# Chunk-selected attention with a gated convolution: the channel order moved into the weights, and seven masks transposed by DMA

## The chip, the cores and the metric

The kernel runs on one core of a Trainium2 chip. The metric is the device time of one launch in microseconds. Engines are called TensorE (PE in the profile, PEld for its weight loads), VectorE (DVE), ScalarE (ACT), GpSimd (POOL) and SyncE (SP), which only issues DMAs here.

## What is computed

Two stages in one launch. The first is causal attention over 4 batches, 8 heads, 768 positions and 64 channels, in which each query may look only at six chunks of 32 keys. The chunks are chosen by an upper bound of the score, made from the smallest and largest key of each chunk. The second stage is a gated linear unit over the 512 channels of all heads: a causal convolution of five taps along the sequence gives a gate for each channel, a matrix product gives a value, and their product goes through an output matrix.

```python
k_min = np.min(k_chunks, axis=3); k_max = np.max(k_chunks, axis=3)
ub = np.sum(np.maximum(q[:, :, :, None, :] * k_min[:, :, None], q[:, :, :, None, :] * k_max[:, :, None]), axis=-1)
ub = np.where(causal, ub, -1e9)
top_chunks = np.argsort(ub, axis=-1)[..., -6:]
scores = scale * np.matmul(q, k.transpose(0, 1, 3, 2))
mask = sel & (pos[:, None] >= pos[None, :])          # sel: the key's chunk is one of the six
scores = np.where(mask, scores, -1e9)
attn = softmax(scores);  attn_out = np.matmul(attn, v)
# ... x = attn_out with the heads side by side: (4, 768, 512)
for k in range(5):
    gate_pre += conv_w[k][None, None, :] * xp[:, k:k + S, :]
gate = 1.0 / (1.0 + np.exp(-gate_pre))
val = x @ w_val
out = (gate * val) @ w_out
```

## The kernel before

The 32 heads are worked on as 16 pairs of heads, p = 0 to 15; four pairs make a batch. All operations are listed with a priority (a stage's offset, plus the pair's number times a period, plus a small correction for each pair), and when the kernel is built a scheduler with a table of costs lays them out into one fixed order for each engine. On the chip each engine runs its list in that order and waits for semaphores where it must. The offsets, the period and the corrections are the numbers PERIOD, OFF and DELTA.

The path of one pair: k and q are loaded and transposed by TensorE (L465), copied out by ScalarE (L471, L507), reduced to chunk bounds by VectorE (L477); GpSimd makes small operands of the bounds (L497 to L502); TensorE makes the upper bounds (L583, or L598 for the first four pairs); VectorE finds the top values and compares (L637, L646), which gives NS, 1 where a chunk is **not** selected. NS must be transposed before it can be used as a penalty:

```python
def selT(p=p):                                             # L656
    b = h16(("sel", p))
    for i in range(NIT):                                   # 5 blocks of 128 x 128
        t.nc.tensor.transpose(out=b[:, i * 128:(i + 1) * 128], in_=vv("NS", p)[:, i, :], identity=t.identh)
def mcopy(p=p):                                            # L662, L664
    if p in EARLY:                                         # pairs 0, 1, 2
        t.nc.scalar.copy(out=vv("MT", p), in_=h16(("sel", p))[:, 0:NIT * 128])
    else:
        t.nc.vector.tensor_copy(out=vv("MT", p), in_=h16(("sel", p))[:, 0:NIT * 128])
```

The scores are two matmuls into the same bank, keys by queries (L678) and then the penalty by MT (L683). ScalarE takes the exponential (L692), GpSimd clears the triangle above the diagonal (L700), TensorE multiplies by v with a column of ones beside it (L721), and VectorE divides by that column. The result is written with channel `32*g + c` at place `4*c + g`, so neighbouring results lie four elements apart:

```python
t.nc.vector.reciprocal(out=rc, in_=b[:, :, D])             # L729
t.nc.vector.tensor_tensor(                                 # L731
    out=vv("on", p).rearrange("q t (c g) -> q t g c", g=4)[:, :, 2 * hh:2 * hh + 2, :],
    in0=b[:, :, 0:D].rearrange("p t (g c) -> p t g c", g=2),
    in1=rc.unsqueeze(2).unsqueeze(3).to_broadcast([128, NT, 2, CH]), op=ALU.mult)
```

`on` is transposed into xT, by TensorE and a VectorE copy (L749, L751) for most pairs, by a DMA transpose for pairs 8 to 14:

```python
t.nc.sync.dma_start_transpose(                             # L754
    out=t.xT[:, p % 8, XL:XL + S].rearrange("c (t q) -> c t q", t=NT),
    in_=vv("on", p).rearrange("q t c -> q (t c)"))
```

For the convolution xT goes through a scratch buffer in DRAM, from which XS takes four channels side by side into one partition (L767, L771); with the order above these are four channels 32 apart. TensorE does the convolution by small diagonal matrices WD (L782), built once from the filter. ScalarE takes a tanh (L788); the value matmuls (L805), gating on VectorE (L813) and output matmuls (L829) follow for each batch.

The weights are loaded to suit that order: w_val by its rows in four strided DMAs, w_out plainly.

```python
def w_val():
    for g in range(4):                                     # L404
        t.nc.gpsimd.dma_start(out=t.wval[g::4], in_=t.w_val.rearrange("(ct g c) e -> g c ct e", g=4, c=32)[g])
def w_out():
    t.nc.gpsimd.dma_start(out=t.wout, in_=t.w_out.rearrange("(et e) o -> e et o", e=128))
```

Of the kernel before, what the change touches and what calls it, by code (L numbers as in the profile page):

```python
# [24 lines left out]
KSZ = 5  # L25
NPAIR = B * H // 2
HB = S // 2
NIT = NT - 1
# [8 lines left out]
SELD = ()  # L37
# [17 lines left out]
for _bi, _segs in enumerate(BANKS):  # L55
    for _col, _jt, _q0, _n in _segs:
        for _i in range(_n // 128):
# [5 lines left out]
PERIOD = 13.9888  # L63
OFF = dict(wdg=365.812, wbig=-412.404, cw=-171.479, load=99.454, ktr=-299.337, qtr=-55.458, kev=-11.458,
           qev=-326.891, ksm=126.528, spl=72.03, vc=306.241, ub=-14.489, top=-212.204, selT=13.558, sc=-46.908,
           ex=-168.011, av=44.528, nrm=91.783, tox=64.078, xs=-89.593, conv=-219.578, tanh=-421.807,
           val=121.402, gv=501.114, out=129.892, ev=145.261)
# [4 lines left out]
EARLY = (0, 1, 2)  # L72
# [6 lines left out]
    wdg=(-4.475, 0, -10.764, -1.987, 2.033, 0, -4.785, -2.614, 0.592, 10.315, -0.932, -0.596, 2.165, -5.612,  # L79
        -6.115, 0),  # L80
    wbig=(0.338, 2.284, 2.312, 3.955, 2.284, 0, 2.359, -3.178, 2.348, 0, 0.237, -0.833, 10.937, 1.375, -0.068,
        0.898),
    cw=(0.01, -4.344, 0, 1.42, 0, 7.277, 3.709, 0, -3.806, 2.37, 9.017, 11.085, 2.915, 1.748, 0, -1.313),
    load=(22.853, 10.481, -1.366, 7.693, -4.489, -0.064, -6.203, 1.08, 14.064, 0.698, -6.083, 0, 0.554, 24.497,
        5.961, 1.331),
    ktr=(-6.278, 1.671, -4.686, 0, -13.252, 0.547, -19.631, 0.094, -1.619, 2.825, 0, 13.211, 0.231, -13.505,
        0.169, 0.169),
    qtr=(0, -2.999, -0.198, -1.684, -0.225, -0.932, -0.697, 5.791, -4.056, 7.187, 0, -6.023, -27.874, 5.254,
        -6.599, 0.947),
    kev=(-2.318, 4.593, -0.511, 7.169, 11.289, -10.745, -0.809, -0.098, 3.8, 1.515, -5.151, 0.867, -0.008,  # L90
        15.747, -2.723, -5.794),
    qev=(-9.704, -0.026, 0.872, -1.066, 0.877, 5.395, 2.396, -2.656, 0, -4.807, -7.099, -6.698, -4.553, 0,
        -8.573, -6.812),
    ksm=(2.968, -0.779, 2.961, -10.575, 5.156, -3.959, -6.512, 0, -2.495, 3.887, -3.949, -0.242, 5.945, 0,
        4.26, 3.885),
    spl=(-3.644, -3.121, 5.651, -5.265, -3.696, 0.587, 0, 0.351, 0.614, 0, -7.431, 2.067, 0.052, 0.506, 0.455,
        0.658),
    vc=(3.53, 0.618, 4.312, -7.064, -1.271, -0.473, 0, 0.387, -2.851, -2.778, -2.789, 0, -3.089, 3.743, -5.236,
        -8.41),
    ub=(-34.616, 8.674, -0.111, 8.208, 11.674, 0.278, 0.154, 1.028, 2.508, 0.474, -2.28, 12.479, 5.429, 11.155,  # L100
        0, -14.798),
    top=(4.06, -2.218, -0.108, -2.736, 3.372, -9.606, -2.777, 0.999, 1.18, 0, 0, 0, 0, -2.663, 0.65, -0.836),
    selT=(-1.343, 0.073, -2.18, -4.611, -19.139, -2.18, -2.256, 6.421, 2.399, 0.067, 0.259, 1.354, -1.984,
        -8.687, 6.579, 0),
    sc=(-1.177, -0.248, 7.153, 1.706, 0, 4.855, 99.574, 2.889, 1.671, 36.583, -4.195, -0.864, 2.658, 7.772,
        8.06, 7.651),
    ex=(4.438, 0, -1.857, 5.99, 7.672, 0, 1.657, -13.074, 22.973, 0, 11.497, 6.699, 9.294, 4.96, 1.319, -6.381),
    av=(-4.883, 0, 16.638, 0.808, 0, 3.656, 0, 2.286, 1.2, -10.459, 0.118, 0.868, 25.013, -20.286, -0.281, 0),
    nrm=(-2.191, -0.406, 2.748, -2.782, 8.522, -3.008, -13.003, -5.319, 7.787, -0.467, -7.559, -3.216, -5.567,
        -6.38, 0, 7.101),  # L110
    tox=(-0.01, 0.016, -25.129, -2.88, -33.605, 0, 5.697, 0.185, 0.682, -3.655, 1.506, 1.493, -4.126, -12.409,
        -17.824, -6.189),
    xs=(2.426, 0, 3.278, 5.577, 4.261, 1.209, 2.648, -15.1, 43.407, -10.841, -2.102, 14.6, -8.246, 1.796,
        -6.886, 1.643),
    conv=(0.165, -7.068, 0, -5.659, -9.164, 0, -1.464, 0, -1.805, 0, 5.265, -1.392, -14.961, 2.661, 0.416,
        -0.681),
    tanh=(6.057, -2.286, -6.723, 0.384, -1.984, 5.971, 1.224, -3.37, 5.788, 4.808, 1.33, 5.008, -1.141, -4.153,
        2.266, -4.981),
    val=(0.564, 5.773, 2.94, 5.419, 10.168, -0.349, 6.821, -105.021, -0.454, 0.57, -23.129, -4.226, -7.487,
        -2.814, 0.39, -1.263),  # L120
    gv=(1.881, 0, -6.009, 2.41, -1.491, -5.581, 4.866, 9.739, 6.248, -1.994, -1.479, 3.901, 0.968, 9.442, 0,
        7.848),
    out=(3.397, -6.947, 0, -12.683, 0, -4.985, -1.525, 0.663, -0.041, 1.671, 2.077, -5.383, -1.07, 0.376,
        -4.172, 0.989),
    ev=(-0.48, 0.806, 3.367, -0.002, 3.796, 5.42, -1.238, 7.536, -3.185, 0, 0, -5.746, 4.018, 0.58, 0.732,
        -9.011),
# [186 lines left out]
def graph(off, period, nbuf):  # L313
# [82 lines left out]
    def w_cw():  # L396
        t.nc.sync.dma_start(out=t.cw, in_=t.conv_w.rearrange("k (c d) -> (k c) d", d=32))
    cwl = G.op("cw", "SP", 0.5, key("cw", 0), w_cw, w=[("cw",)], dma=0.1)

    later, last = [], []  # L400
    def w_val():

        for g in range(4):
            t.nc.gpsimd.dma_start(out=t.wval[g::4], in_=t.w_val.rearrange("(ct g c) e -> g c ct e", g=4, c=32)[g])  # L404
    last.append(G.op("wval", "POOL", 2.0, key("wbig", 2), w_val, w=[("wval",)], dma=3.2))

    def w_out():
        t.nc.gpsimd.dma_start(out=t.wout, in_=t.w_out.rearrange("(et e) o -> e et o", e=128))
    last.append(G.op("wout", "POOL", 1.0, key("wbig", 4), w_out, w=[("wout",)], dma=3.2))

    def w_rep():
        for r in range(2):
            t.nc.vector.tensor_copy(out=t.cw4[:, r], in_=t.cw.unsqueeze(2).to_broadcast([80, 32, 2]))
    cwr = G.op("cwrep", "DVE", 0.3, key("cw", 0), w_rep, r=[("cw",)], w=[("cw4",)])

    def w_tr():
        t.nc.tensor.transpose(out=bank("cwT")[:, 0:80], in_=t.cw4.rearrange("p r d b -> p (r d b)"),
                              identity=t.ident[0:80, 0:80])
    G.op("cwT", "PE", 0.15, key("cw", 2), w_tr, r=[("cw4",), ("ident",)], w=[("cwT",)], ps=["cwT"])
# [21 lines left out]
    for p in range(NPAIR):  # L441
# [211 lines left out]
        def selT(p=p):  # L653
            b = h16(("sel", p))
            for i in range(NIT):
                t.nc.tensor.transpose(out=b[:, i * 128:(i + 1) * 128], in_=vv("NS", p)[:, i, :], identity=t.identh)  # L656
        G.op(f"selT{p}", "PE", 0.28, key("selT", p), selT, r=[("NS", p), ("identh",)], w=[("selT", p)],
             war=[("MT", p)], ps=[("sel", p)])
# [6 lines left out]
        G.op(f"mc{p}", *(("ACT", act(640)) if p in EARLY else ("DVE", dve(640, 2))), key("selT", p), mcopy, r=[("selT", p)], w=[("MT", p)], ps=[("sel", p)])  # L665
# [59 lines left out]
        def norm(hh, p=p):  # L725
            def emit():
                b = bank(("av", p, hh))[:, 0:NT * (D + 1)].rearrange("p (t d) -> p t d", t=NT)
                rc = t.rcp[(p * 2 + hh) % 4]
                t.nc.vector.reciprocal(out=rc, in_=b[:, :, D])  # L729

                t.nc.vector.tensor_tensor(  # L731
                    out=vv("on", p).rearrange("q t (c g) -> q t g c", g=4)[:, :, 2 * hh:2 * hh + 2, :],
                    in0=b[:, :, 0:D].rearrange("p t (g c) -> p t g c", g=2),
                    in1=rc.unsqueeze(2).unsqueeze(3).to_broadcast([128, NT, 2, CH]), op=ALU.mult)
            return emit
# [193 lines left out]
def kernel(  # L929
# [18 lines left out]
    def tl(name, shape, dt=FP):  # L948
        return cp.tile(shape, dt, tag=name, name=name)
# [12 lines left out]
    t.cw = tl("cw", [80, 32])  # L962
    t.cw4 = tl("cw4", [80, 2, 32, 2])
# [6 lines left out]
    t.scr = [dr.tile([2, 128, XH], F16, tag=f"scr{i}", name=f"scr{i}") for i in range(4)]  # L970
    t.wval = tl("wval", [128, NCT, DM], F16)
# [47 lines left out]
```

## Time and profile before

| | |
|---|---|
| Time, median of 3 runs | 196.15 us (196.0 to 198.43) |
| Span of the profiled execution | 194.4 us, 7664 instructions |
| Granted TensorE clock | full speed throughout |
| DMA | 37.64 MB, mean 194 GB/s; 82,192 of 92,468 packets under 512 bytes |
| SyncE's DMA queue | 81.9% of the time of 16 DMA engines |

How to read it: a row of the groups gives line, engine, operation, output and inputs with their shapes, the count, then busy time and mean ns of one instruction, then the idle time of the engine just before it and what ended that. Rows of neighbouring instructions of one engine overlap in time (the next one starts while the last is still finishing), so a row's mean is longer than what the engine gives to it; the step from one start to the next is the better measure. The chain is followed back from the last instruction, at each step to whatever released it. A "landing" of a DMA is the time from its issue to the arrival of its data.

### The profile page before, as it was taken

What the parts mean: (1) busy time and instruction counts of PE and PEld (TensorE: products, weight loads), DVE (VectorE), ACT (ScalarE), POOL (GpSimd) and SP (SyncE); (2) the same over time, 40 slices, a digit from 0 to 9 for tenths busy, and PEclk for the clock granted to TensorE, in tenths of its full rate; (3) what the DMA queues carried; (4) which work ended last, traced back from release to release, by engine and by line L of the source; (5) the groups of instructions that cost most, each with busy time, mean ns of one, the idle gap of its engine ahead of it and who ended that gap; (6) DMA issues with size and microseconds to landing.
All of it is one profiled execution on the core that took longest, in us unless ns stands there. A gap on an engine that the chain in (4) does not pass through costs nothing.

```text
span 194.4 us, 7664 instructions
## 1 busy us (share of the span) xinstructions
PE 182.0 (94%) x3026; PEld 121.5 (63%) x3026; DVE 151.5 (78%) x459; ACT 145.3 (75%) x326; POOL 86.0 (44%) x183
## 2 busy tenths in 40 slices
PE   7979999799999989999999999999899999799992
PEld 2766768577667656566677566677658566444540
DVE  4596998999988989987999899699987742714441
ACT  4659999988789579688989764997889898073421
POOL 5236999977462635454456521526362341000000
PEclk9999999999999999999999999999999999999999
DMA  6999999999399949999898998698971396855425
GB/s 145 218 218 205 222 205 200 216 161 284 81 214 237 237 98 222 254 225 227 174 260 172 135 227 227 162 222 229 140 259 63 57 235 184 259 194 185 165 108 216
DMA packets 92468, 37.64 MB, mean 194 GB/s; under 512 B 82192, under 2 KB 87312, under 8 KB 92432
## 3 DMA queue, kind: packets, MB, share of 16 engines
q1 hardware_dynamic: 91328, 36.10, 81.9%
q0 software_dynamic: 1104, 1.05, 3.9%
q8 instruction: 24, 0.39, 0.9%
q14 instruction: 12, 0.10, 0.2%
HBM read 27.34 MB, written 9.47 MB: 189 GB/s over the span
## 4 chain that ended last, share of the span: by engine, by line
PE 52%; DVE 31%; ACT 7%; DMA 4%; issue 3%; POOL 2%; SPq 0%; ACTq 0%; DVEq 0%; POOLq 0%
PE b L829 11%; PE b L805 8%; DVE on L731 7%; DVE km L477 7%; PE b L782 6%; PE b L678 6%; PE b L721 5%; PE b L465 4%; PE b L683 4%; DVE rl L553 3%; ACT P L692 3%; PE b L583 3%; DVE ql L515 3%; DMA XS<-scr 2%; DVE top L637 2%
## 5 line engine op out<-in xcount | busy, mean ns | idle before, releaser
L692 ACT ACTIVATE P<-b 128x512 f16<-128x512 f32 (+1 forms) x192 | 89.6, 605 | 4.9 <-PE b L683 3.0
L700 POOL TENSOR_SCALAR_AFFINE_SELECT P<-P 128x512 f16<-128x512 f16 (+1 forms) x64 | 35.4, 574 | 44.4 <-ACT P L692 44.4
L678 PE MATMUL b<-Qh,Kh 64*128 64x128 f16 (+3 forms) x384 | 41.7, 259 | 1.4 <-DVE on L731 1.2
L683 PE MATMUL b<-MT,E 64*128 64x128 f16 (+4 forms) x352 | 37.6, 255 | 0.1
L477 DVE TENSOR_REDUCE km<-b 128x12 f32<-128x384 f32 x64 | 32.0, 546 | 5.8 <-PE b L465 5.1
L731 DVE TENSOR_TENSOR on<-b,rcp 128x384 f16<-128x384 f32 x32 | 32.8, 1024 | 1.2
L813 DVE SCALAR_TENSOR_TENSOR gv<-g,b 128x384 f16<-128x384 f32 x32 | 17.0, 551 | 14.9 <-PE b L805 14.3
L721 PE MATMUL b<-VA,P 128*128 128x65 f16 x672 | 27.3, 194 | 0.7 <-DVE on L731 0.7
L721 PEld LDWEIGHTS <-P 128*128 128x128 f16 x672 | 24.3, 98 | 5.2 <-issue 3.7
L788 ACT ACTIVATE g<-b 128x384 f32<-128x384 f32 x32 | 14.1, 501 | 17.7 <-PE b L782 17.7
L678 PEld LDWEIGHTS <-Kh 64*128 64x128 f16 x384 | 18.5, 94 | 13.2 <-issue 9.0
L805 PE MATMUL b<-xT,wval 128*128 128x384 f16 x128 | 24.0, 327 | 0.0
L829 PE MATMUL b<-wout,gv 128*128 128x512 f16 x96 | 23.2, 380 | 0.2 <-DVE on L731 0.2
L839 ACT ACTIVATE osb<-b 128x512 f32<-128x512 f32 x21 | 12.7, 613 | 12.6 <-PE b L829 8.8
L683 PEld LDWEIGHTS <-E 64*128 64x128 f16 x352 | 17.9, 94 | 5.8 <-issue 3.1
L471 ACT ACTIVATE Kh<-b 128x384 f16<-128x384 f32 x32 | 16.4, 532 | 4.7 <-PE b L465 2.8
L507 ACT ACTIVATE Qh<-b 128x384 f16<-128x384 f32 x32 | 14.9, 523 | 3.6 <-PE b L465 3.6
L782 PE MATMUL b<-XS,WD 64*32 64x384 f16 x640 | 16.1, 324 | 1.0 <-DMA XS<-scr 1.0
L553 DVE SCALAR_TENSOR_TENSOR rl<-Qh,ql 128x640 f16<-128x640 f16 x16 | 15.4, 964 | 1.9 <-ACT ql L530 1.8
L805 PEld LDWEIGHTS <-wval 128*128 128x128 f16 x128 | 11.3, 98 | 8.3 <-issue 1.1
L497 POOL TENSOR_TENSOR km<-km 128x24 f32<-128x24 f32 x16 | 5.5, 346 | 23.8 <-DVE km L477 23.8
L570 POOL CAST VA<-vn 128x768 f16<-128x768 f32 x16 | 13.7, 864 | 4.1 <-PE b L721 4.1
(86 smaller groups left out, 302.5 us busy)
## 6 DMA issues: line engine op xcount, KB each, us to landing
XS<-scr SPq DMA_DIRECT2D x32, 194.0 KB, 4.1
kn<-in_k_dram SPq DMA_DIRECT2D x32, 192.0 KB, 4.4
qn<-in_q_dram SPq DMA_DIRECT2D x32, 192.0 KB, 4.5
vn<-in_v_dram SPq DMA_DIRECT2D x16, 384.0 KB, 6.0
out_dram<-osb SPq DMA_DIRECT2D x24, 256.0 KB, 2.2
scr<-xT SPq DMA_DIRECT2D x32, 97.0 KB, 3.7
wval<-in_moe_w_val_dram POOLq DMA_DIRECT2D x4, 128.0 KB, 4.7
wout<-in_moe_w_out_dram POOLq DMA_DIRECT2D x1, 512.0 KB, 7.5
```

The source lines that it names most:

```text
L477: t.nc.vector.tensor_reduce(out=vv("km", p)[:, i, w * 12:(w + 1) * 12], in_=bank(("kn", p, w))[:, 0:HB].rearrange("p (c t) -> p c t", t=CH ...
L553: t.nc.vector.scalar_tensor_tensor(out=vv("rl", p), in0=vv("Qh", p)[:, 128:S], scalar=0.0, in1=vv("ql", p), op0=ALU.is_gt, op1=ALU.mult)
L678: nc.tensor.matmul(out=bb[hh][:, col:col + n], lhsT=kh[HP[hh], jt * 128:(jt + 1) * 128], rhs=qh[HP[hh], q0:q0 + n], start=(si == 0), stop= ...
L683: nc.tensor.matmul(out=bb[hh][:, col + m0 - q0:col + n], lhsT=t.E[HP[hh], jt * 128:(jt + 1) * 128], rhs=mt[HP[hh], m0 - 128:q0 + n - 128], ...
L692: t.nc.scalar.activation(out=t.P[p % 2][hh][bi], in_=bank(("s", p, bi, hh))[:, 0:n], func=AF.Exp, scale=0.125 / QS)
L700: t.nc.gpsimd.affine_select(out=ap, in_=ap, pattern=[[0, n], [1, 128]], compare_op=ALU.is_ge, fill=0.0, base=0, channel_multiplier=-1)
L721: t.nc.tensor.matmul(out=b[:, qt, :], lhsT=t.P[p % 2][hh][bi][:, col:col + 128], rhs=vv("VA", p)[:, hh, jt, :], start=(jt == 0), stop=(jt ...
L731: t.nc.vector.tensor_tensor(out=vv("on", p).rearrange("q t (c g) -> q t g c", g=4)[:, :, 2 * hh:2 * hh + 2, :], in0=b[:, :, 0:D].rearrange ...
L782: t.nc.tensor.matmul(out=bank(("cv", p, r))[32 * g:32 * g + 32, 0:HB], lhsT=t.WD[HP[r], k * 16 + (p % 4) * 4 + g, :], rhs=x[HP[r], g * XH ...
L805: t.nc.tensor.matmul(out=k[:, 0:HB], lhsT=t.wval[:, ct, et * 128:(et + 1) * 128], rhs=t.xT[:, (4 * b_ + ct) % 8, XL + w * HB:XL + (w + 1) ...
L813: t.nc.vector.scalar_tensor_tensor(out=vv("gv", 4 * b_ + et)[:, sl], in0=vv("g", 4 * b_ + et)[:, sl], scalar=1.0, in1=bank(("val", b_, et, ...
L829: t.nc.tensor.matmul(out=k, lhsT=vv("gv", 4 * b_ + et)[:, s * 128:(s + 1) * 128], rhs=t.wout[:, et, :], start=(et == 0), stop=(et == NCT - 1))
```

## The change

Two things are changed, and the order of work was then laid out anew.

First, the norm writes its channels in their own order. The regrouping that the convolution needs is put elsewhere: four neighbouring channels `4*c + g` now lie side by side in a partition of XS, and the convolution gives its result with `g` outermost. So the filter's diagonals are built in another order, the columns of w_val are permuted within each block of 128 by four GpSimd copies, and the rows of w_out are loaded by four strided DMAs.

Second, for pairs 9 to 15 the mask NS is transposed into MT by one DMA transpose on SyncE's queue, and not by five TensorE transposes and a VectorE copy.

```diff
-SELD = ()
+SELD = range(9, NPAIR)
-PERIOD = 13.9888
+PERIOD = 13.2487
 # ... nearly all of OFF and DELTA has new numbers
-        t.nc.sync.dma_start(out=t.cw, in_=t.conv_w.rearrange("k (c d) -> (k c) d", d=32))
+        t.nc.sync.dma_start(out=t.cw, in_=t.conv_w.rearrange("k (e q) -> (k e) q", q=128))
     def w_val():
-        for g in range(4):
-            t.nc.gpsimd.dma_start(out=t.wval[g::4], in_=t.w_val.rearrange("(ct g c) e -> g c ct e", g=4, c=32)[g])
+        t.nc.gpsimd.dma_start(out=t.wvn, in_=t.w_val.rearrange("(ct c) e -> c ct e", c=128))
+    def w_perm(ct):
+        return lambda: t.nc.gpsimd.tensor_copy(out=t.wval[:, ct].rearrange("p (e g c) -> p e g c", e=NCT, g=4),
+                                               in_=t.wvn[:, ct].rearrange("p (e c g) -> p e g c", e=NCT, g=4))
     def w_out():
-        t.nc.gpsimd.dma_start(out=t.wout, in_=t.w_out.rearrange("(et e) o -> e et o", e=128))
+        for g in range(4):
+            t.nc.gpsimd.dma_start(out=t.wout[32 * g:32 * g + 32], in_=t.w_out.rearrange("(et c g) o -> g c et o", g=4, c=32)[g])
     def w_rep():
         for r in range(2):
-            t.nc.vector.tensor_copy(out=t.cw4[:, r], in_=t.cw.unsqueeze(2).to_broadcast([80, 32, 2]))
+            t.nc.vector.tensor_copy(out=t.cw4[:, :, r], in_=t.cw.rearrange("p (c g) -> p g c", g=4).unsqueeze(3).to_broadcast([20, 4, 32, 2]))
     def w_tr():
-        t.nc.tensor.transpose(out=bank("cwT")[:, 0:80], in_=t.cw4.rearrange("p r d b -> p (r d b)"),
-                              identity=t.ident[0:80, 0:80])
+        for g in range(4):
+            t.nc.tensor.transpose(out=bank("cwT")[:, 20 * g:20 * g + 20], in_=t.cw4[:, g].rearrange("p r c b -> p (r c b)"),
+                                  identity=t.ident[0:20, 0:20])
+        def mdma(p=p):
+            t.nc.sync.dma_start_transpose(out=vv("MT", p).rearrange("c (t q) -> c t q", t=NIT),
+                                          in_=vv("NS", p).rearrange("q t c -> q (t c)"))
+        if p in SELD:
+            G.op(f"md{p}", "SP", 1.1, key("selT", p), mdma, r=[("NS", p)], w=[("MT", p)], dma=0.8, tail=1.5)
+        # ... else: transposes and copy as before
-                t.nc.vector.tensor_tensor(
-                    out=vv("on", p).rearrange("q t (c g) -> q t g c", g=4)[:, :, 2 * hh:2 * hh + 2, :],
-                    in0=b[:, :, 0:D].rearrange("p t (g c) -> p t g c", g=2),
-                    in1=rc.unsqueeze(2).unsqueeze(3).to_broadcast([128, NT, 2, CH]), op=ALU.mult)
+                t.nc.vector.tensor_tensor(out=vv("on", p)[:, :, hh * 64:(hh + 1) * 64], in0=b[:, :, 0:D],
+                                          in1=rc.unsqueeze(2).to_broadcast([128, NT, D]), op=ALU.mult)
-                                           lhsT=t.WD[HP[r], k * 16 + (p % 4) * 4 + g, :],
+                                           lhsT=t.WD[HP[r], g * 20 + k * 4 + p % 4, :],
```

More of the change, by code (lines that the diff above doesn't have):

```diff
@@ L61 @@
             MT=2, on=2, xT=8, XS=3, g=8, gv=8, osb=4, scr=4)
-PERIOD = 13.9888
[L64 to L67, printed above, removed]
+PERIOD = 13.2487
+OFF = dict(wdg=689.463, wbig=-821.57, cw=-638.386, load=-26.611, ktr=-313.189, qtr=-239.905, kev=166.913,
+           qev=-383.955, ksm=148.208, spl=244.528, vc=540.922, ub=-278.308, top=-291.823, selT=-172.354,
+           sc=-256.234, ex=-198.66, av=-117.315, nrm=263.685, tox=-134.594, xs=14.333, conv=-269.157,
+           tanh=-393.525, val=323.303, gv=522.471, out=327.173, ev=91.258)
 EARLY = (0, 1, 2)
@@ L78 @@
 DELTA = dict(
[L79 to L124, printed above, removed]
@@ L125 @@
-    ev=(-0.48, 0.806, 3.367, -0.002, 3.796, 5.42, -1.238, 7.536, -3.185, 0, 0, -5.746, 4.018, 0.58, 0.732,
-        -9.011),
+    wdg=(-0.259, 11.176, 5.417, 0.077, -1.668, 4.13, 5.35, 1.029, 15.805, 3.045, -3.731, 0, -3.953, 0, 0, 0),
+    wbig=(4.521, -1.173, -4.251, -0.71, -6.836, -7.879, -1.406, -13.108, -0.554, -12.202, 1.098, -1.574,
+        -2.473, -1.919, 10.286, 15.067),
+    cw=(0, 0, 1.049, 0, -3.776, -0.311, -0.92, -4.993, -0.92, -6.529, -7.915, -11.168, 0.948, 0, -8.06, 3.706),
+    load=(-9.433, -20.842, -32.131, -6.001, -15.044, -1.827, -12.02, 13.514, 5.014, 13.589, 14.754, 5.081,
+        -6.414, 4.609, -2.48, -7.659),
@@ new lines @@
+    ktr=(-2.8, -5.035, -2.262, 2.581, 0.902, 9.564, 0, 0, 10.923, 1.13, -0.491, -0.903, 0, 13.091, 0, -1.519),
+    qtr=(0, -0.071, 9.102, 0, 3.757, 12.574, 5.717, -4.881, -3.114, -14.91, -6.366, 2.222, 0.471, 9.573, 4.53,
+        0),
+    kev=(-2.229, -2.16, 2.677, -4.88, -7.568, -10.347, 4.307, -2.668, 4.622, 3.276, -0.858, 6.192, 2.689,
+        -4.962, -5.387, -2.214),
+    qev=(-4.798, -6.316, 0, 0.959, 0, -3.801, -4.226, -3.069, -0.528, -1.223, 0, 0, -6.763, 0, 2.363, 0.065),
+    ksm=(13.028, 3.364, 1.499, 0.759, -1.548, -11.855, -3.051, 6.295, -16.352, 0.972, -0.612, 7.732, 0, -1.146,
+        0, -2.064),
@@ new lines @@
+    spl=(1.262, 11.137, -16.05, -1.69, -4.33, -6.699, -40.483, 4.206, 3.281, 19.318, -19.036, -16.32, 12.261,
+        -5.656, 10.037, 0.718),
+    vc=(1.748, -27.085, -4.307, 0, -5.756, -0.371, -4.158, 0.266, 21.35, -3.576, 0, 0.35, 5.25, -0.034, 12.327,
+        7.302),
+    ub=(-1.261, -1.704, -7.813, 3.091, -4.015, -14.948, 0, 2.233, 2.322, 0, -7.876, 13.15, -8.595, -0.126,
+        -18.872, -17.052),
+    top=(5.067, 2.169, 6.094, 9.602, 14.045, 13.01, -0.156, -5.897, 1.098, 0.084, 2.913, 2.943, 2.121, -0.002,
+        0, 11.724),
@@ new lines @@
+    selT=(10.026, 2.182, -0.498, 4.774, -0.189, -0.821, 5.123, 1.014, 0.873, 3.056, 12.093, 5.215, 1.134,
+        -0.467, -2.246, 0.26),
+    sc=(-3.684, 2.323, 6.111, 6.751, -2.871, -17.678, -30.23, -1.526, -13.134, -1.219, 1.476, -1.084, 0.465,
+        26.912, 1.856, -0.962),
+    ex=(0.518, -1.916, 26.612, -0.555, 1.908, 0, -0.304, 1.658, -12.071, 1.68, 0, -4.112, -1.281, 0, -6.681,
+        3.816),
+    av=(8.141, 23.715, 0, -3.234, 0.925, 0.036, -16.039, -1.518, -0.512, -1.918, -1.793, -11.122, 7.414, 0,
+        4.536, 0.431),
@@ new lines @@
+    nrm=(0.219, -0.69, -2.27, -15.358, -3.955, -5.17, 1.725, 5.097, 2.136, 76.904, 10.773, 11.399, 0.327,
+        10.314, 6.848, 16.568),
+    tox=(5.083, -9.624, -3.531, 16.222, -3.29, 7.771, 0.127, 7.218, -3.237, 2.083, -3.821, -1.177, 0.557,
+        -9.325, 3.562, 1.286),
+    xs=(-0.589, -20.407, -3.618, 3.816, 0, -1.25, 2.952, -7.384, 2.493, 1.773, 2.46, -0.962, -12.556, 1.62,
+        -0.613, 2.66),
+    conv=(-0.411, -7.384, -5.199, -0.916, -1.613, -3.484, 2.127, -5.739, 0, 0, 3.767, 12.228, 5.66, -7.854,
+        6.314, 3.519),
@@ new lines @@
+    tanh=(-0.597, 0.252, -0.042, 6.877, 0, 0, 20.177, 16.64, 2.504, 0.308, 20.302, -0.547, 4.277, 0.743, 5.404,
+        6.23),
+    val=(0.746, 0, 0, -4.309, -5.054, 0.632, 3.993, -168.145, 0, 0, 4.124, 1.076, -6.197, -6.958, -8.508,
+        -6.597),
+    gv=(5.505, -3.972, 0, 7.879, 16.599, -0.597, 3.312, -14.616, -0.18, 0, 4.163, 0.738, 0.401, -3.09, -5.366,
+        4.144),
+    out=(-0.646, 3.026, -0.113, -7.77, -3.659, 3.789, 4.916, -4.962, 2.461, 0, -1.067, 11.205, -13.796, -2.374,
+        -0.072, 0.251),
@@ L127 @@
+    ev=(9.081, -6.619, 0.125, -22.323, 0, 0, -4.231, -5.332, 22.655, 3.336, 2.632, -2.286, -26.622, -11.207,
+        4.364, 10.267),
 )
@@ L401, in w_val, with w_out @@
     def w_val():
-        for g in range(4):
-            t.nc.gpsimd.dma_start(out=t.wval[g::4], in_=t.w_val.rearrange("(ct g c) e -> g c ct e", g=4, c=32)[g])
-    last.append(G.op("wval", "POOL", 2.0, key("wbig", 2), w_val, w=[("wval",)], dma=3.2))
-    def w_out():
-        t.nc.gpsimd.dma_start(out=t.wout, in_=t.w_out.rearrange("(et e) o -> e et o", e=128))
-    last.append(G.op("wout", "POOL", 1.0, key("wbig", 4), w_out, w=[("wout",)], dma=3.2))
+        t.nc.gpsimd.dma_start(out=t.wvn, in_=t.w_val.rearrange("(ct c) e -> c ct e", c=128))
+    last.append(G.op("wval", "POOL", 1.0, key("wbig", 2), w_val, w=[("wvn",)], dma=3.2))
+    def w_perm(ct):
+        return lambda: t.nc.gpsimd.tensor_copy(out=t.wval[:, ct].rearrange("p (e g c) -> p e g c", e=NCT, g=4),
+                                               in_=t.wvn[:, ct].rearrange("p (e c g) -> p e g c", e=NCT, g=4))
+    for ct in range(NCT):
+        G.op(f"wperm{ct}", "POOL", 0.8, key("wbig", 3, ct), w_perm(ct), r=[("wvn",)], w=[("wval",)])
+    def w_out():
+        for g in range(4):
+            t.nc.gpsimd.dma_start(out=t.wout[32 * g:32 * g + 32], in_=t.w_out.rearrange("(et c g) o -> g c et o", g=4, c=32)[g])
+    last.append(G.op("wout", "POOL", 2.0, key("wbig", 4), w_out, w=[("wout",)], dma=3.2))
     def w_rep():
         for r in range(2):
-            t.nc.vector.tensor_copy(out=t.cw4[:, r], in_=t.cw.unsqueeze(2).to_broadcast([80, 32, 2]))
-    cwr = G.op("cwrep", "DVE", 0.3, key("cw", 0), w_rep, r=[("cw",)], w=[("cw4",)])
+            t.nc.vector.tensor_copy(out=t.cw4[:, :, r], in_=t.cw.rearrange("p (c g) -> p g c", g=4).unsqueeze(3).to_broadcast([20, 4, 32, 2]))
+    cwr = G.op("cwrep", "DVE", 0.7, key("cw", 0), w_rep, r=[("cw",)], w=[("cw4",)])
     def w_tr():
-        t.nc.tensor.transpose(out=bank("cwT")[:, 0:80], in_=t.cw4.rearrange("p r d b -> p (r d b)"),
-                              identity=t.ident[0:80, 0:80])
-    G.op("cwT", "PE", 0.15, key("cw", 2), w_tr, r=[("cw4",), ("ident",)], w=[("cwT",)], ps=["cwT"])
+        for g in range(4):
+            t.nc.tensor.transpose(out=bank("cwT")[:, 20 * g:20 * g + 20], in_=t.cw4[:, g].rearrange("p r c b -> p (r c b)"),
+                                  identity=t.ident[0:20, 0:20])
+    G.op("cwT", "PE", 0.3, key("cw", 2), w_tr, r=[("cw4",), ("ident",)], w=[("cwT",)], ps=["cwT"])
     def w_split():
@@ L656, in selT @@
                 t.nc.tensor.transpose(out=b[:, i * 128:(i + 1) * 128], in_=vv("NS", p)[:, i, :], identity=t.identh)
-        G.op(f"selT{p}", "PE", 0.28, key("selT", p), selT, r=[("NS", p), ("identh",)], w=[("selT", p)],
-             war=[("MT", p)], ps=[("sel", p)])
+        def mdma(p=p):
[3 more added lines that the diff above has]
+            G.op(f"md{p}", "SP", 1.1, key("selT", p), mdma, r=[("NS", p)], w=[("MT", p)], dma=0.8, tail=1.5)
+        else:
+            G.op(f"selT{p}", "PE", 0.28, key("selT", p), selT, r=[("NS", p), ("identh",)], w=[("selT", p)],
+                 war=[("MT", p)], ps=[("sel", p)])
         def mcopy(p=p):
@@ L664, in mcopy @@
                 t.nc.vector.tensor_copy(out=vv("MT", p), in_=h16(("sel", p))[:, 0:NIT * 128])
-        G.op(f"mc{p}", *(("ACT", act(640)) if p in EARLY else ("DVE", dve(640, 2))), key("selT", p), mcopy, r=[("selT", p)], w=[("MT", p)], ps=[("sel", p)])
+        if p not in SELD:
+            G.op(f"mc{p}", *(("ACT", act(640)) if p in EARLY else ("DVE", dve(640, 2))), key("selT", p), mcopy, r=[("selT", p)], w=[("MT", p)], ps=[("sel", p)])
         def score(bi, p=p):
@@ L961 @@
     t.E = tl("E", [128, S], F16)
-    t.cw = tl("cw", [80, 32])
-    t.cw4 = tl("cw4", [80, 2, 32, 2])
+    t.cw = tl("cw", [20, 128])
+    t.cw4 = tl("cw4", [20, 4, 2, 32, 2])
     t.pm = tl("pm", [128, 2])
@@ L970 @@
     t.scr = [dr.tile([2, 128, XH], F16, tag=f"scr{i}", name=f"scr{i}") for i in range(4)]
+    t.wvn = tl("wvn", [128, NCT, DM], F16)
     t.wval = tl("wval", [128, NCT, DM], F16)
```

## The prediction, made before the changed kernel had run

> **What bounds the kernel now.** I read the page's first part first, then busy time by stretch, then the chain that ended last, then the groups of the lines that the diff touches, and last the order of single instructions in one stretch. The page by engine, and the four stretches that I cut the span into (columns: length, then busy us and count of PE, PEld, DVE, ACT, POOL, then granted clock, DMA share, GB/s):
>
> ```profile
> PE 182.0 (94%) x3026; PEld 121.5 (63%) x3026; DVE 151.5 (78%) x459; ACT 145.3 (75%) x326; POOL 86.0 (44%) x183
> 0.00:26.00 26.00, 22.96 (x297) 15.93 (x298) 19.02 (x73) 18.81 (x43) 15.12 (x38) 1.00 1.12 203
> 26.00:85.00 59.00, 55.39 (x1025) 40.23 (x1026) 54.78 (x157) 49.59 (x115) 38.05 (x76) 1.00 0.95 201
> 85.00:143.00 58.00, 57.13 (x962) 38.47 (x958) 53.11 (x168) 47.54 (x109) 24.93 (x56) 1.00 0.96 200
> 143.00:194.40 51.40, 46.51 (x747) 26.91 (x746) 24.62 (x64) 29.33 (x64) 7.94 (x16) 1.00 0.55 173
> ```
>
> The reader is to see three stages: a head of 26 us, a middle of 117 us in which VectorE is busy 107.9 us (54.78 + 53.11, 92%), and a tail of 51 us in which VectorE is idle half the time and TensorE alone sets the pace. TensorE's 94% must not be taken at its word: its rows overlap. In the order of single instructions five mask transposes of L656 begin at 87.89 and the next operation at 88.18, so they take 0.29 us, though their merged row spans 0.45. With such start-to-start steps (L721 0.032 each, L805 0.163, L829 0.216, L782 0.94 for 40, L583 0.69 for 20, L465 0.68 for 6, some 2.3 us of scores for a pair) the middle holds about 100 us of TensorE work in 117: 86%. So in the middle VectorE is the fullest engine, TensorE and ScalarE (97.1 us, 83%) are close behind, and the chain says the same:
>
> ```profile
> PE 52%; DVE 31%; ACT 7%; DMA 4%; issue 3%; POOL 2%; SPq 0%; ACTq 0%; DVEq 0%; POOLq 0%
> ```
>
> Of those 31%, L731 (the norm) is 7% and L477 another 7%. The listed waits of TensorE on VectorE are each about a microsecond or less: many small hand-overs, not one stall.
>
> The groups that the diff touches, and three to hold them against (busy us, mean ns | idle before):
>
> ```profile
> L731 DVE TENSOR_TENSOR on<-b,rcp 128x384 f16<-128x384 f32 x32 | 32.8, 1024 | 1.2
> L813 DVE SCALAR_TENSOR_TENSOR gv<-g,b 128x384 f16<-128x384 f32 x32 | 17.0, 551 | 14.9 <-PE b L805 14.3
> L477 DVE TENSOR_REDUCE km<-b 128x12 f32<-128x384 f32 x64 | 32.0, 546 | 5.8 <-PE b L465 5.1
> L646 DVE TENSOR_TENSOR NS<-mub,top 128x240 f16<-128x240 f32 x12 | 5.3, 445 | 0.0
> L664 DVE COPY MT<-b 128x640 f16<-128x640 f16 x13 | 6.4, 489 | 1.8 <-PE b L656 1.7
> L656 PE MATMUL b<-identh,NS 128*128 128x128 f16 x80 | 7.2, 220 | 0.8 <-DVE NS L646 0.7
> ```
>
> The norm takes 1024 ns where two other operations that read 384 fp32 elements from PSUM take about 550. It differs in two things: one operand is broadcast, and its fp16 results are written four elements apart. The broadcast isn't to blame: L646 has a broadcast operand too and runs at a median of 400 ns for 240 elements, on the same line as the others. That leaves the spread-out write.
>
> **What the skill says.** The page "SBUF — State Buffer", in "Door 1: The DMA port swizzle (why [64,N] ≈ [32,N])", says that SBUF works in lines of 16 bytes, that two or more accesses to a line keep full bandwidth, and that one may stride freely up to 8 bf16 elements. The write here is 8 bytes apart, two to a line, so by that rule it should be free; the 1024 ns against 551 say otherwise, and I go with the trace. "VectorE: DVE Perf Modes", "The three transpose paths", gives 390 ns for a 128x128 transpose on TensorE, into PSUM, and 1309 ns through the DMA crossbar, into SBUF. The trace's TensorE transposes are 220 ns long and 58 ns apart, and six 128x128 blocks together go through one DMA with a 3.7 us landing, so neither figure is usable as a rate. "DMA: Bandwidth & Descriptors", "Issuing engines are not separate DMA queues", says that all DMAs share the same 16 engines. The trace agrees insofar as the DMA share is 0.95 in the middle with all kinds of transfer mixed. The page "Perfetto Trace Analysis", "Identifying the Most-Contended Engine", warns that matmul busy time is a poor measure; the 0.29 against 0.45 us above is a case of it.
>
> **The change part by part.**
>
> *Norm without the spread.* The channel order goes into the weights, and the norm writes 64 adjacent elements. Rows on VectorE overlap, so I count start to start: in the stretch at 95 us
>
> ```profile
> 95.46 1.01 DVE L731 TENSOR_TENSOR on<-b,rcp 128x384 f16<-128x384 f32 x1
> 96.28 0.43 DVE L646 TENSOR_TENSOR NS<-mub,top 128x240 f16<-128x240 f32 x1
> ...
> 98.67 0.48 DVE L664 COPY MT<-b 128x640 f16<-128x640 f16 x1
> 99.07 1.47 DVE L477 TENSOR_REDUCE km<-b 128x12 f32<-128x384 f32 x3
> ```
>
> a norm holds the engine 0.82 us (95.46 to 96.28); four reduces in the chain take 1.86 us, 0.465 each. I expect the new norm at about 550 ns by row and 0.46 by step: 0.36 us saved, 32 times, 11.5 us in all. Of these 24 lie in the middle: 8.6 us of the fullest engine there.
>
> *Masks of pairs 9 to 15 by DMA.* Seven times five transposes (0.29 us) go from TensorE, 2.0 us, and seven copies at 0.40 us (98.67 to 99.07) from VectorE, 2.8 us; some five pairs lie in the middle, so 1.5 and 2.0 us there. A PSUM bank per pair is freed as well. Added are seven DMA transposes of 128x640 fp16, 164 KB each. The model for them is the transpose of the outputs that is there already:
>
> ```profile
> L754 SPq DMA_TRANSPOSE xT<-on x7: 1210/1296/3054, 107.1 to 160.5; - x7
> xT<-on SPq DMA_TRANSPOSE x7, 3.7
> ```
>
> So 1.3 us of SyncE's queue each, 9.1 us together, and 3 to 4 us from issue to landing, where transposes and copy took about 1.9 us (transposes at 97.27, copy begun at 98.67 and 0.48 long). The order of work is laid out anew to hide that.
>
> *Weights.* w_val becomes one DMA and four GpSimd copies, w_out four DMAs in place of one: five issues before and after. A 768-element cast on GpSimd (L570) is 826 ns, so four 512-element copies are 2.2 us, up to 4 us if their strided reads are slow. GpSimd is busy 38 of 59 us in the second stretch and the first use of w_val (L805) is at 65 us: hidden. The filter's set-up grows: two copies of 256 elements in place of 64 and four small transposes in place of one, about +0.4 us on VectorE, once, near 20 us.
>
> *The order itself.* Nearly all offsets are new. The kernel's own table counts a norm pair of operations at 0.697 us in both versions; before, the trace has 0.187 + 1.024. With the new norm (0.187 + 0.55) the table is about right, so the laid-out order should hold better on the chip. I give that no number of its own.
>
> *Sum.* In the middle VectorE drops from 107.9 to about 97.3 us (-8.6 - 2.0), TensorE from 100 to 98.5, ScalarE stays at 97.1. All three are then level. If the fullest is again at 92% of its stretch, the middle is 98.5 / 0.92 = 107 us, 10 less. The tail has one path through a norm (163 to 165 us, before the XS transfer): -0.5. The head +0.4. DMA and the longer mask latency should take back about 0.5. Together -9.6: 196.15 becomes **186.5 us**.
>
> **Rivals.** *DMA or SyncE's queue becomes the bound.* For it: the share of 0.95, and SyncE's issues fill 47 of the 58 us from 85 to 143; some 9 us more make 56. Against it: the loads run up to five pairs ahead, DMA is only 4% of the chain, part of the issue time is waiting for a full queue, and slices of the page reach 237 to 284 GB/s where the mean is 194. If it holds, half the gain goes: 190 to 192 us. *Mask latency shows.* Two microseconds more for each of seven pairs, with TensorE in order behind L683, would cost up to 14 us if nothing lay between; with an order built for it I expect far less, but a third of it would leave 191. *The write isn't the cause,* and the norm stays near 1 us: only the masks' 2 to 3 us of VectorE and the new order are left, 193 to 195. *The new order fits better than I count:* TensorE's work is about 156 us in all by the same steps, so 179 to 181 is within reach if the head and the gaps shrink too.
>
> **Range and chances.** The upper end is the DMA rival, the lower the last one: **180 to 192**. Faster by over 2% needs less than 192.2, which only several rivals together forbid: **0.86**; within 2% **0.11**; slower **0.03**.
>
> **What would show it.** The norm's group near 550 ns and VectorE near 138 us in all; the mask copies at six in place of thirteen; VectorE's share in the middle no more than TensorE's; the chain with less VectorE and more TensorE; seven more DMA transposes with landings of 3 to 5 us and few TensorE waits on them. The prediction is wrong if L683 or its weight load waits on a DMA for several microseconds, if transposes to TensorE of k and q wait on loads, if the norm keeps its 1 us, or if the tail grows by what the middle gives up.

## The result, and the profile after

The changed kernel takes a median of 190.24 us (188.03 to 191.3, 4 runs) against 196.07 (195.46 to 198.43, 4 runs). The ratio is **0.9632**, with a 95% interval of 0.9544 to 0.9721. The ratio rests on the two shorter of these four executions (188.03 and 189.31 us, hence its wide interval) and stands for some 188.9 us, while the profile below is of one of the two longer ones (191.16 us), although all four ran at the full granted clock. Faster was right, the size fell short: 186.5 was predicted.

The page by engine and the same four stretches as before (columns: length, busy us and count of PE, PEld, DVE, ACT, POOL, granted clock, DMA share, GB/s), then the chain by engine:

```profile
PE 177.9 (94%) x2994; PEld 118.3 (62%) x2994; DVE 138.0 (73%) x452; ACT 145.3 (77%) x326; POOL 88.1 (46%) x187
26.00:85.00 59.00, 57.79 (x1071) 41.59 (x1068) 52.60 (x174) 51.68 (x119) 39.79 (x82) 1.00 0.95 210
85.00:143.00 58.00, 58.00 (x1020) 39.65 (x1018) 50.26 (x175) 51.34 (x117) 29.41 (x63) 1.00 1.07 202
143.00:189.50 46.50, 39.39 (x608) 21.15 (x604) 15.26 (x33) 22.66 (x49) 3.60 (x7) 1.00 0.76 204
```

```profile
PE 68%; DMA 9%; ACT 7%; DVE 5%; POOL 5%; issue 2%; SPq 2%; ACTq 0%; DVEq 0%; POOLq 0%
```

VectorE's share of the chain has gone from 31% to 5%, TensorE's from 52% to 68%. In the two middle stretches VectorE is down from 107.9 to 102.9 us though more work goes through (349 of its instructions in place of 325), ScalarE is up from 97.1 to 103.0, and from 85 to 143 us no gap is left on TensorE's row.

The groups of the lines that were changed (busy us, mean ns | idle before):

```profile
L744 DVE TENSOR_TENSOR on<-b,rcp 128x384 f16<-128x384 f32 x32 | 17.8, 558 | 1.1
L824 DVE SCALAR_TENSOR_TENSOR gv<-g,b 128x384 f16<-128x384 f32 x32 | 17.1, 549 | 15.6 <-PE b L816 13.9
L677 DVE COPY MT<-b 128x640 f16<-128x640 f16 x6 | 2.9, 490 | 0.5 <-ACT P L706 0.3
L663 PE MATMUL b<-identh,NS 128*128 128x128 f16 x45 | 4.0, 219 | 0.7 <-DVE NS L653 0.6
```

The norm is at 558 ns, level with the gating (549). Seven mask copies and 35 transposes are gone. The masks by DMA, and the last comparisons that make them (from the views of the tiles MT and NS; duration ns min/median/max, then first and last start; L646 is the kernel before):

```profile
L665 SPq DMA_TRANSPOSE MT<-NS x7: 1215/1306/2277, 90.6 to 146.7; - x7
DMA to landing us min/median/max: 3.4/4.2/5.3
L653 DVE TENSOR_TENSOR NS<-mub,top x12: 397/400/814, 43.6 to 142.2; 128x240 f16<-128x240 f32 x12
L646 DVE TENSOR_TENSOR NS<-mub,top x12: 393/400/882, 47.0 to 149.3; 128x240 f16<-128x240 f32 x12
```

The waits list has no wait of TensorE on a mask's DMA at all. The last comparison is a useful milestone, since the same work lies before it in both kernels: it starts at 142.2 us, where before it started at 149.3. So in these two executions 7.1 us were gained up to there, and 2.2 were given back between there and the end (45.1 us before, 47.3 after): 4.9 us in all, where the ratio stands for 7.2. Whether the 2.2 us belong to the change is taken up below.

### The profile page after: what moved, and what is told of

Same layout as the page of the kernel before. It is cut to its first block, busy times and chain, and to the rows that moved or that the text cites. A ratio compares the mean times of both kernels' runs of the same rounds, so it can differ in the third digit from the quotient of the medians.

```text
span 189.5 us, 7611 instructions
## 1 busy us (share of the span) xinstructions
PE 177.9 (94%) x2994; PEld 118.3 (62%) x2994; DVE 138.0 (73%) x452; ACT 145.3 (77%) x326; POOL 88.1 (46%) x187
## 4 chain that ended last, share of the span: by engine, by line
PE 68%; DMA 9%; ACT 7%; DVE 5%; POOL 5%; issue 2%; SPq 2%; ACTq 0%; DVEq 0%; POOLq 0%
PE b L735 10%; PE b L692 9%; PE b L840 9%; PE b L816 9%; PE b L472 9%; PE b L793 8%; DMA XS<-scr 7%; PE b L697 6%; PE b L590 5%; ACT P L706 4%; DMA qn<-in_q_dram 2%; DVE km L484 1%; PE b L663 1%; ACT Qh L514 1%; PE b L760 1%
## 5 line engine op out<-in xcount | busy, mean ns | idle before, releaser
L706 ACT ACTIVATE P<-b 128x512 f16<-128x512 f32 (+2 forms) x192 | 88.8, 593 | 6.2 <-PE b L697 2.1
L714 POOL TENSOR_SCALAR_AFFINE_SELECT P<-P 128x512 f16<-128x512 f16 (+1 forms) x64 | 33.9, 551 | 44.9 <-ACT P L706 44.8
L692 PE MATMUL b<-Qh,Kh 64*128 64x128 f16 (+3 forms) x384 | 39.8, 259 | 0.6 <-ACT P L706 0.6
L697 PE MATMUL b<-MT,E 64*128 64x128 f16 (+4 forms) x352 | 36.9, 255 | 0.1
L692 PEld LDWEIGHTS <-Kh 64*128 64x128 f16 x384 | 17.6, 94 | 12.8 <-issue 8.0
L697 PEld LDWEIGHTS <-E 64*128 64x128 f16 x352 | 17.3, 94 | 4.7 <-issue 2.0
L744 DVE TENSOR_TENSOR on<-b,rcp 128x384 f16<-128x384 f32 x32 | 17.8, 558 | 1.1
L560 DVE SCALAR_TENSOR_TENSOR rl<-Qh,ql 128x640 f16<-128x640 f16 x16 | 14.6, 911 | 2.2 <-ACT ql L537 2.2
L472 PE MATMUL b<-ident,qn 128*128 128x128 f32 x96 | 14.7, 281 | 0.5 <-ACT P L706 0.3
L472 PE MATMUL b<-ident,kn 128*128 128x128 f32 x96 | 14.4, 283 | 0.5 <-DMA kn<-in_k_dram 0.3
```

Source lines behind the costliest of these rows:

```text
L472: t.nc.tensor.matmul(out=b[:, j * 128:(j + 1) * 128], lhsT=vv(name, p)[:, 3 * w + j, :], rhs=t.ident, is_transpose=True, start=(j == 0), s ...
L692: nc.tensor.matmul(out=bb[hh][:, col:col + n], lhsT=kh[HP[hh], jt * 128:(jt + 1) * 128], rhs=qh[HP[hh], q0:q0 + n], start=(si == 0), stop= ...
L697: nc.tensor.matmul(out=bb[hh][:, col + m0 - q0:col + n], lhsT=t.E[HP[hh], jt * 128:(jt + 1) * 128], rhs=mt[HP[hh], m0 - 128:q0 + n - 128], ...
L706: t.nc.scalar.activation(out=t.P[p % 2][hh][bi], in_=bank(("s", p, bi, hh))[:, 0:n], func=AF.Exp, scale=0.125 / QS)
L714: t.nc.gpsimd.affine_select(out=ap, in_=ap, pattern=[[0, n], [1, 128]], compare_op=ALU.is_ge, fill=0.0, base=0, channel_multiplier=-1)
L744: t.nc.vector.tensor_tensor(out=vv("on", p)[:, :, hh * 64:(hh + 1) * 64], in0=b[:, :, 0:D], in1=rc.unsqueeze(2).to_broadcast([128, NT, D]) ...
```

## The experiments

### Is it the norm's time? The norm alone, in both orders

Two runs hold each engine's order exactly and change only how the norm writes. In `e1_flat_norm`, the kernel before with the results side by side:

```diff
-    out=vv("on", p).rearrange("q t (c g) -> q t g c", g=4)[:, :, 2 * hh:2 * hh + 2, :],
+    out=vv("on", p)[:, :, hh * 64:(hh + 1) * 64].rearrange("q t (g c) -> q t g c", g=2),
```

> The kernel before with one edit: the norm writes its 64 results side by side, through the same broadcast operand and the same pattern of reads; weights, masks and order of work stay, so the channel order of the output no longer fits the weights and only the time is of use. Theory A (VectorE's time in the norm carries the gain): norm rows near 0.55 us in place of 1.02, time 188.5 to 190.5. Theory B (the new order of work carries it): 194 to 196. Theory C (the masks by DMA carry it): 194 to 196.

Measured: 190.22 us, ratio to before 0.9715 (0.9663 to 0.9767). In `e2_spread_norm_in_after`, the changed kernel with the norm of the kernel before (the reverse of the last hunk on the norm in the diff):

> The changed kernel with one edit: the norm writes four elements apart again (the weights stay in the new order, so the output's channels don't fit them). Theory A: back to 195 to 198, with VectorE the fullest engine of the middle again. Theory B or C: the gain stays, 190 to 192.

Measured: 194.15 us, ratio 0.9892 (0.9861 to 0.9922). In the old order the norm is worth 2.85%, in the new one 2.6% (0.9632 / 0.9892 = 0.974). The two agree, so the norm's part stands by itself, and it is the largest part. In e2 VectorE is again at 108.4 of the 117 us of the middle, and the scores on TensorE wait for the norm again (1.5 us). What is left, masks and order and weights together, is worth 1.1% with the slow norm (e2, clear of noise) and 0.9% with the fast one (0.9632 / 0.9715 = 0.991, where the two intervals overlap). Theory A is right in kind; its 195 to 198 for e2 left this remainder out.

### Why was the norm slow? The spread of the writes

`e8_spread_of_writes` is the kernel before with another spread in each of four groups of pairs:

```diff
-    g=4 for all pairs
+    p % 4 == 0: side by side (4-dimensional pattern kept); 1: g=2; 2: g=4; 3: g=8
```

> The kernel before with the norm's results written side by side in pairs 0, 4, 8, 12, two elements apart in pairs 1, 5, 9, 13, four apart in 2, 6, 10, 14 and eight apart in 3, 7, 11, 15 (the channel order of the output no longer fits). If each new 16-byte line costs a fixed time once fewer than two results fall into it: 0.56, 0.56, 1.02 and more than 1.02 us or the same. If any spread leaves a slow path: 0.56 and three times about 1.02. If the 4-dimensional pattern and not the spread were the cause: 1.02 for the first, 0.56 for the second.

The view of the tile `on` in the one execution that was taken (min/median/max ns), with the four lines in this order:

```profile
L732 DVE TENSOR_TENSOR on<-b,rcp x8: 556/557/558, 26.0 to 152.0; 128x384 f16<-128x384 f32 x8
L737 DVE TENSOR_TENSOR on<-b,rcp x8: 586/592/602, 36.1 to 154.0; 128x384 f16<-128x384 f32 x8
L742 DVE TENSOR_TENSOR on<-b,rcp x8: 1016/1027/1036, 42.7 to 160.0; 128x384 f16<-128x384 f32 x8
L747 DVE TENSOR_TENSOR on<-b,rcp x8: 1854/1872/1892, 51.2 to 167.8; 128x384 f16<-128x384 f32 x8
```

The pattern's dimensions don't matter (557 with four of them) and two elements apart is nearly free. From there the time nearly doubles with each doubling of the distance: 845 ns more from eight to sixteen bytes for the same 384 results. The first expectation fits best. In the 16-byte lines of the Trainium skill ("SBUF — State Buffer", "Door 1: The DMA port swizzle (why [64,N] ≈ [32,N])") the 384 results fall into 192 lines at eight bytes and 384 at sixteen, so 845 / 192 = 4.4 ns for each further line, an estimate. By that, 96 lines at four bytes cost 0.42 us, less than the 0.46 us that a reduce of 384 elements takes from start to start, so they would not show. The page's threshold of two accesses to a line is not enough for these writes; four were. A cost that grows with the distance itself would give the same four durations up to sixteen bytes; only a wider step would tell the two apart, and no run has one. That the spread is the cause is shown, the line as its unit is not.

### Which engine bounds the middle? Work taken from TensorE, before and after

Both kernels without most of the penalty matmuls (L683, in the changed kernel L697) of pairs 3 to 11, so those masks are mostly not applied. By start-to-start steps that is some 0.9 us for a pair, and 8 us for the nine (an estimate):

```diff
-    masked = m0 < q0 + n
+    masked = m0 < q0 + n and not (3 <= p <= 11 and bi > 0)
```

> The kernel before with the penalty matmuls of pairs 3 to 11 left out except in the first score bank, so that the masks of those pairs are mostly not applied; about 8 us of TensorE work go, nearly all of it in the middle, nothing else. If VectorE bounds the middle before: 193 to 196, a quarter or less of the 8 us shows. If TensorE bounds it: 188 to 190.

> The changed kernel with the same penalty matmuls left out as in e10. If TensorE bounds the middle after the change: 182 to 185, most of the 8 us shows. If DMA or the SyncE queue bounds it: 188 to 190.5, the time of the changed kernel.

Measured: before 196.13 us, ratio 1.0006 (0.9984 to 1.0028): taking 8 us of TensorE work away does **nothing** to the kernel before. So TensorE did not bound its middle; with e1, where less VectorE time brings 2.85% in the same order, this shows VectorE as the bound. After, 187.01 us, ratio 0.9534 (0.9506 to 0.9561) against 0.9632 (0.9544 to 0.9721) for the changed kernel: about 1%, 2 us of the 8, and by the ends of the two intervals anything from nothing to half of the 8. So neither outcome that I had written for e11 is right. The chain of e11 and its middle stretches:

```profile
PE 56%; DVE 15%; ACT 14%; DMA 7%; issue 4%; SPq 3%; ACTq 0%; DVEq 0%
26.00:85.00 59.00, 57.02 (x1011) 40.12 (x1009) 54.20 (x178) 52.99 (x123) 41.64 (x84) 1.00 1.02 222
85.00:143.00 58.00, 57.08 (x962) 38.22 (x962) 49.78 (x175) 51.95 (x120) 28.37 (x60) 1.00 1.02 201
```

The reader is to see ScalarE at 104.9 of 117 us and VectorE at 104.0, both near 90%, and in the chain VectorE rises from 5 to 15% and ScalarE from 7 to 14%. After the change three engines are nearly level, and taking work from TensorE alone is worth little.

### Do the masks by DMA help? Swapped with every order held

If the masks' transposes are added to or taken from the list of operations, the scheduler lays everything out anew. Three runs avoid this. In `e6_old_order_masks_swapped` (on e1) and `e5_new_order_masks_swapped` (on e3, below) the order is that made for masks by TensorE, and at the place of each transpose of pairs 9 to 15 a DMA is issued:

```diff
+    if p in range(9, NPAIR):        # in selT; mcopy returns at once for these pairs
+        t.nc.sync.dma_start_transpose(out=vv("MT", p)..., in_=vv("NS", p)...)
+        return
```

> The kernel of e1 (old order, norm side by side), with the masks of pairs 9 to 15 swapped in place as in e5. Theory C1: 2 us of TensorE work less where TensorE is the fullest engine, 187.5 to 189 against 190.2. Theory C2: 190 to 192, no gain, or a loss where L683 comes to wait for the DMA.

> The kernel of e3, every engine's order held as it is there (laid out for masks by TensorE), but the five transposes and the copy of each of pairs 9 to 15 are left out of the two engines and one DMA transpose stands at their place. If the 5 us between e3 and the changed kernel are the work of TensorE and VectorE that the masks take away (theory C1): 190 to 191.5. If they come from the order that is laid out differently with the masks by DMA (theory C2): 194 to 196, or slower if the longer mask latency shows, since this order was not made for it.

Measured: e6 199.8 us, ratio 1.0157 (1.0075 to 1.0238), against 0.9715 for e1. And e5 200.61 us, ratio 1.0243 (1.0186 to 1.0301), against 0.9939 for e3. Put into an order not made for them, the seven DMAs cost 3 to 4.5%. The waits of TensorE (us in total, times, longest) in e6:

```profile
PE b L690 <- DMA MT<-NS: 7.8, 4, 3.7
```

And in e5:

```profile
PE b L704 <- DMA MT<-NS: 5.0, 4, 2.5
```

A part of the landing, which is 2.8 us by the median in e6 and 3.8 in e5, stands bare on TensorE in four of the seven pairs. In e6 the granted clock falls after the longer gaps as well, so part of the loss is slower matmuls. The stretches around the gap that ends at 107.34 us (columns as above, the clock is third from the end):

```profile
104.00:106.00 2.00, 0.20 (x4) 0.08 (x5) 1.82 (x4) 0.87 (x2) 1.14 (x3) 1.00 1.03 161
106.00:108.00 2.00, 0.66 (x12) 0.46 (x12) 0.00 (x0) 0.15 (x1) 0.89 (x3) 1.00 1.07 96
108.00:110.00 2.00, 2.00 (x16) 1.26 (x14) 0.55 (x1) 1.53 (x3) 1.23 (x2) 0.66 1.05 238
110.00:112.00 2.00, 2.00 (x12) 0.81 (x10) 1.09 (x3) 1.65 (x4) 0.00 (x0) 0.50 1.18 228
```

In the reverse, `e13_new_order_masks_back`, the changed kernel's order is held and the masks of these pairs go back to TensorE and VectorE, between the place of the DMA and the first use:

```diff
-    t.nc.sync.dma_start_transpose(out=vv("MT", p)..., in_=vv("NS", p)...)
+    # at a place where a bank is free, before the first score matmul of the pair
+    5 x t.nc.tensor.transpose(out=b[...], in_=NS[:, i, :], identity=t.identh)
+    t.nc.vector.tensor_copy(out=MT, in_=b[:, 0:NIT * 128])
```

> The changed kernel with every engine's order held, but the mask of each of pairs 9 to 15 is transposed by TensorE and copied by VectorE, put into the two lists where a PSUM bank is free between the place of the DMA and the first use of the mask; the seven DMA transposes are left out. If the masks by DMA are worth their TensorE and VectorE time in the order made for them: 2 us of TensorE and 2.8 us of VectorE come back where all engines are nearly full, 190.5 to 193. If what they bring is only that the order was made with them: 188 to 190.5.

Measured: 190.84 us, ratio 0.9729 (0.9684 to 0.9774), against 0.9632 (0.9544 to 0.9721). That is 1% for the masks by DMA where the order hides them, as much as the 2.0 us of TensorE time, but the two intervals overlap and the medians (190.84 and 190.24) are only 0.6 us apart. So it is shown that the masks by DMA cost nothing to speak of in the order made for them, and not shown that they gain.

### The parts by themselves, with the order laid out anew

These runs do the whole computation with one part taken out or put in, and the scheduler runs again on the changed list.

```diff
 e3_masks_by_tensore:           changed kernel, SELD = ()
 e4_new_order_alone:            kernel before, PERIOD, OFF and DELTA of the changed one
 e7_norm_and_masks_old_numbers: changed kernel, PERIOD, OFF and DELTA of the kernel before
```

> The changed kernel with the masks of pairs 9 to 15 transposed by TensorE and copied by VectorE again; norm, weights and the numbers of the order stay as changed. Theory A: 189.5 to 191.5, within 1% of the changed kernel, since only 2.8 us of VectorE and 2 us of TensorE come back. Theory C: 193 to 196.

> The kernel before with the new numbers of the order (period, offsets, corrections) and nothing else: spread-out norm, masks by TensorE. Theory A: 194 to 199, no gain, since the norm's 1.02 us remain. Theory B: 190 to 192.

> The changed kernel with the numbers of the order (period, offsets, corrections) of the kernel before; norm, weights and masks as changed. If the new numbers matter beside the two other parts: 192 to 195. If they don't: 189 to 191, the time of the changed kernel.

Measured: e3 195.49 us, 0.9939 (0.9912 to 0.9967); e4 202.56 us, 1.0342 (1.0318 to 1.0365); e7 193.11 us, 0.9858 (0.9814 to 0.9901). Read naively, e3 says that masks by DMA bring 3% and e7 that the new numbers bring 2%, together more than the whole change. Both contradict the runs with held orders, where the masks bring about 1% and masks, order and weights together 0.9 to 1.1%. The reading that fits all of them is that the numbers were fitted to one list of operations, and that with another list the order that comes out is worse. Three pairs of runs show that the order alone moves the time, since each pair does the same work in two orders: e3 takes 2.1% longer than e13 (0.9939 / 0.9729, intervals apart), e4 3.4% longer than the kernel before, and e7 2.3% longer than the changed kernel. My expectations for e3 and e4 fell, and these three runs measure orders and not the parts.

### What does the weights' set-up cost?

`e12_norm_and_weights_only` is the kernel before with the norm and all the weights' set-up of the change, in the old order, masks by TensorE; the four GpSimd copies follow two casts of v:

```diff
+    if p in (4, 5):                 # in vcast
+        2 x t.nc.gpsimd.tensor_copy(out=t.wval[...permuted...], in_=t.wvn[...])
```

> The kernel before with the norm side by side and the weights set up as in the change, each engine's old order held (the four GpSimd copies of w_val follow two casts of v near 48 and 57 us), masks by TensorE. The whole computation is done. If the weights' set-up is hidden: 189.5 to 191, as e1. If it costs: 191 to 193.

Measured: 191.69 us, ratio 0.9777 (0.9754 to 0.98), against 0.9715 for e1: about 0.6%, 1.2 us, with intervals that overlap a little, so it is likely and not settled. The view of the tile cw and the waits of TensorE show one part of it:

```profile
L413 DVE COPY cw<-cw x2: 711/804/898, 19.6 to 20.2; 20x256 f32<-20x256 f32 x2
PE b L418 <- DVE cw L413: 0.8, 1, 0.8
```

Two copies of 0.80 us stand where two of 0.40 were, and TensorE waits for them. In the changed kernel's own order the copies take as long but no engine is listed as waiting for them, so the 1.2 us are the price in the old order.

## Why the prediction was right, and where it fell short

*VectorE bounds the middle.* Right, shown by e10 and e1 together.

*The spread-out write is the cause, and 550 ns the new time.* Right: 558 ns, and e8 shows the spread to be the cause. VectorE in all was to fall to about 138 us and is at 138.0.

*TensorE, ScalarE and VectorE are then level.* Right: VectorE 102.9 and ScalarE 103.0 us in the middle, and e11 shows that freeing TensorE alone brings about a quarter of the freed time, half at the most.

*The fullest engine is again at 92%, so the middle shrinks by 10 us.* This is the term that was mis-sized. From 26 us to the last comparison it was 123.3 us and is 116.2 in the profile: 7.1 less. With the 98.5 us of TensorE work that I counted for 117 us, that is 98.5 / (117 x 116.2 / 123.3) = 89%, an estimate. That one full engine can be kept at 92% by the others' slack, while three level ones wait for each other more, is my reading of it; no run tests it. e1 says the same with one part alone: 2.85% of 196 is 5.6 us, where I had put 8.6 us on the path for the norm.

*The tail gains 0.5.* Not seen: in the profile of the changed kernel it is 2.2 us longer. The waits list names the largest part, the way of the attention's result through DRAM to the convolution:

```profile
PE b L793 <- DMA XS<-scr: 3.3, 3, 1.3
```

Before, this wait came once, for 1.0 us. But two other profiles in the changed kernel's order don't show the loss. The last comparisons of e2 and e13, in this order:

```profile
L653 DVE TENSOR_TENSOR NS<-mub,top x12: 399/404/820, 45.9 to 148.2; 128x240 f16<-128x240 f32 x12
L653 DVE TENSOR_TENSOR NS<-mub,top x12: 393/398/817, 43.4 to 144.7; 128x240 f16<-128x240 f32 x12
```

With spans of 193.2 and 188.7 us their tails are 45.0 and 44.0 us, and the wait is 0.4 us in e2 and, in e13, 0.4 us on a weight load alone; e11 has 46.3 us with 2.4 us of it. So the tail grows with this wait, and the 2.2 us are not shown to belong to the change. Why the wait comes in some profiles and not in others stays open.

*Weights: hidden but for 0.4 us.* The GpSimd part was near the low end of my estimate (four copies of 0.66 us), the copies of the filter took 0.8 us more in place of 0.4, and the whole came to about 1.2 us in the old order (e12).

*Masks and order.* I gave the masks 1.5 us of TensorE and 0.5 back; e13 puts the masks at about 1%, 2 us, not clear of noise. I gave the new order no number of its own. e12 and e13 do the same work in the old and the new order, and e13 is 0.5% shorter, within the noise. e5 and e6 show that an order made for them is the condition for the masks: without it, the masks by DMA cost 6 to 9 us. The rival "mask latency shows" was thus real and had been provided for. The rival of a full DMA or SyncE queue did not come to pass in the middle, though the DMA share rose to 1.07 from 85 to 143 us: no listed wait of TensorE on a load of k or q is above 0.3 us.

Step by step, each by ratios of 196 us: the norm 5.6 us (e1), the weights 1.2 us back (from e1 to e12), masks and order together 2.8 us (from e12 to the changed kernel, 0.9777 to 0.9632). That is 7.2 in place of the 9.6 of my sum. That the sum came so near is in part luck: the norm brought about 3 us less than I had counted, while masks and order brought 2.8 where I had counted about 1.

## What to carry to other kernels

When an engine bounds a stage, look for operations of it that take longer than others of the same size, and hold the access patterns side by side before counting operations. Once one engine's excess is gone and the next ones are level with it, don't expect all of the saved time: here the norm's 11.5 us (counted by steps) became 5.6. In a kernel with a fixed order, a part can be priced only with the order held: a new list of operations is a new order, and its effect, 2 to 3.4% here, covers what is to be measured.

## What the runs showed of the hardware

- VectorE's fp16 writes of 384 results took 557, 592, 1027 and 1872 ns with the results 2, 4, 8 and 16 bytes apart (e8).
- A DMA transpose of 128x640 fp16 within SBUF took 1.2 to 1.4 us of SyncE's queue by the median and, over the runs, 2.6 to 5.3 us to land. Seven of them, each put in place of TensorE's 0.29 us without a new order, made the kernel 3 to 4.5% slower (e5, e6).
- After 3.14 us in which TensorE stood idle, its granted clock in the next stretches of 2 us was 0.66 and 0.50, before it was back at 0.99 (e6).
